# The opening of a long-convolution kernel: k's first chunk and its taps placed ahead of the filter, and kv transposed in 16-bit instead of 32-bit words

## The chip, the cores and the metric

One core of a Trainium2 chip runs the whole program. The metric is the device time of one execution in microseconds (us), median of several runs. The engines are named as in the profile: PE (TensorE matmul, with PEld for its weight loads), DVE (VectorE), ACT (ScalarE), POOL (GpSimd) and SP (SyncE, which only issues DMAs here). ACTq, DVEq and SPq are the instruction queues of those engines.

## The reference

Inputs are q, k, v (1 x 2048 x 512, bf16), a tap filter shift_k (512 x 4), a long filter ssm_k (512 x 2048), a vector ssm_D (512), and the weights w1 (512 x 1376), w2 (1376 x 512).

```python
k_shift = sum over t of k_pad[:, t:t+S, :] * shift_k[:, ks-1-t]   # 4 causal taps per channel
kv = k_shift * v
y  = irfft(rfft(kv, 2S) * rfft(ssm_k, 2S))[:S] + kv * ssm_D       # long causal convolution
h  = x + layernorm(x) * y                                          # x = q
h2 = h + relu(layernorm(h) @ w1) @ w2
```

The result is h2, in bf16.

## The kernel before, in words

The convolution is a transform of length 4096 in two stages of matmuls, 64 x 64, for the filter and for kv alike, with channels spread over the 128 partitions in four groups of 128 (`DC` = 4). The order of the instructions on each engine is written out by hand (`manual_schedule`); a framework adds the semaphores. PE works through these steps, in this order:

1. Transposes of ssm_k (`to_rows`, L246, on `sk`): eight groups of eight 128x128 transposes of 16-bit data. Each group fills one buffer of PSUM (`pst`) and is copied to `kfl` by DVE or ACT in turn (the letters "DADADADA", L291).
2. Eight rounds (L315 to L319). Round `gb` first computes one tap group (`taps`, L303): for a chunk of 512 tokens `c = gb // 2` and half of the channels, 8 matmuls of `kT` with diagonal matrices `wdiag` into `pkv`, and DVE multiplies the result by `vT` in two instructions (L310). The products kv go into `sk`, whose old content is used up by then, in pairs of neighbouring tokens. Then stage 1 of the filter for group `gb` (`stage1`, L252): 64 small matmuls into two buffers, copied to `a1k` by ACT, or by ACT and DVE in odd groups. After groups 0, 2 and 4, ACT also computes a piece of the cosine table `c2c` (`cc_part`, L210); the first of its four pieces comes ahead of step 1.
3. Transposes of kv (L337 to L349): each pair of 16-bit tokens is taken as one 32-bit word, so 32 transposes do; DVE copies a buffer as int32 words, ACT as 16-bit values in two instructions. The result is `xfl`.
4. Stage 2 of the filter (L281, L283, buffers `ps2k`, result `kf`), stage 1 of kv (`a1x`), the products of the spectra (L398), the inverse transform (L528 and L592), and the two layers of the network (`ps1m`, L604; `ps2m`, L621).

Four PSUM buffers of two banks each (`psF`, tag "ps") go round among all tiles of steps 1 to 4. A tile takes the buffer that was used four tiles earlier and waits until that one has been copied out.

SP issues, one after the other: ssm_k into `sk` (L95), then for each chunk `c` a transposing DMA of k (`kT`, L111 and L113) and one of v (`vT`, L114). ACT's queue issues shift_k (`wsh`, L97) and ssm_D (`draw`, L102) first. POOL builds `wdiag` from an identity and `wsh` (L222), then the small tables `f1hi` and `f1lo` that stage 1 multiplies by, and the negated sine table `c2n` (L229). DVE computes the turns (integers, `tsn` and `tcs`) from which ACT makes the tables by its sine function; `tcs`, the cosine's, is computed ahead of all copies (L206). `dm_f` (L205), a small table for the inverse, is the last that ACT makes before the cosine's first piece. `a1k` and later large tiles share one slot of SBUF, `slotA`: what is written into it waits for the readers of what was there before.

## Time and profile before

| | |
|---|---|
| median of 3 runs | 218.69 us (217.52 to 219.26) |
| profiled execution, its own time | 217.52 us |
| its span, first to last instruction | 215.7 us |
| granted TensorE clock | 1.000 |
| PE busy | 194.0 us (90%) |
| DVE, ACT, POOL busy | 143.3, 115.8, 79.4 us |
| ssm_k, issue to landing | 8.2 us |
| k chunks, v chunks, median issue to landing | 6.6, 5.7 us |

The profile shows one execution. Busy time of an engine counts only where that engine is what others wait for; the chain that ended last follows the work back from the last instruction and says at each step what released it. Times of instructions are counted from the start of the span. The time of an execution is somewhat longer than its span, since it includes what lies before the first and behind the last instruction that the profile records.

### The profile page before, as it was taken

The page shows a single profiled execution, that of the slowest core. Times are in us where ns is not written, and L with a number is a line of the kernel's source. Part 1 is how long each engine was busy: PE and PEld are TensorE (multiplying, and loading weights), DVE is VectorE, ACT ScalarE, POOL GpSimd, SP SyncE. Part 2 cuts the span into 40 slices and gives each one's busy share as a digit, 9 for nine tenths or more (in the row PEclk, how much of TensorE's full clock was granted, in tenths as well). Part 3 has the DMA queues.
Part 4 walks back from the last instruction along what each step waited for, and adds up shares of the span by engine and source line. Part 5 has one row for each costly group of instructions (what it writes and reads, how often), then busy time and mean ns, then how long its engine had stood idle before and what let it go on. Part 6 is the DMA issues. An engine that isn't in the chain of part 4 may idle for free.

```text
span 215.7 us, 5459 instructions
## 1 busy us (share of the span) xinstructions
PE 194.0 (90%) x2251; PEld 137.2 (64%) x2267; DVE 143.3 (66%) x236; ACT 115.8 (54%) x177; POOL 79.4 (37%) x120
## 2 busy tenths in 40 slices
PE   0399879899997999998998999999999999999992
PEld 0385434799986899996998944654646644444451
DVE  7965756976697999998495991988395470243031
ACT  2976848745697788883997048202450047016400
POOL 3299992000002999995747702110201010002000
PEclk9999999999999999999999999999999999999999
DMA  6999950000000006809950799494462430010012
GB/s 194 317 208 197 154 127 3 5 5 0 0 5 3 0 3 173 269 14 214 178 100 0 266 148 148 79 185 95 85 114 52 100 79 3 24 49 24 0 47 55
DMA packets 49513, 20.08 MB, mean 93 GB/s; under 512 B 44400, under 2 KB 47952, under 8 KB 49488
## 3 DMA queue, kind: packets, MB, share of 16 engines
q1 hardware_dynamic: 46816, 18.18, 41.4%
q10 hardware_dynamic: 2672, 1.54, 2.5%
q8 instruction: 18, 0.29, 0.6%
q14 instruction: 7, 0.06, 0.1%
HBM read 7.08 MB, written 2.10 MB: 43 GB/s over the span
## 4 chain that ended last, share of the span: by engine, by line
PE 83%; DVE 9%; DMA 4%; issue 2%; ACT 1%; DVEq 0%; ACTq 0%
PE ps1m L604 18%; PE ps2m L621 18%; PE psi L528 7%; PE psy L408 7%; PE pkv L307 7%; PE pz L592 5%; DVE a1x L241 4%; DMA sk<-in_A_ssm_k_dram 4%; PE ps2k L281 3%; PE ps2k L283 3%; PE u L281 3%; PE u L283 3%; PE pst L249 3%; PE ps L265 3%; PE pst L340 2%
## 5 line engine op out<-in xcount | busy, mean ns | idle before, releaser
L606 ACT ACTIVATE h1T<-ps1m 128x512 bf16<-128x512 f32 (+1 forms) x44 | 26.0, 596 | 55.4 <-PE ps1m L604 55.4
L621 PE MATMUL ps2m<-w,h1T 128*128 128x512 bf16 (+2 forms) x179 | 38.6, 366 | 0.6 <-issue 0.3
L604 PE MATMUL ps1m<-xT,w 128*128 128x512 bf16 (+1 forms) x176 | 38.8, 379 | 0.3 <-DVE xT L577 0.3
L624 DVE SCALAR_TENSOR_TENSOR o<-ps2m,rstd,xh 128x512 bf16<-128x512 f32 (+1 forms) x17 | 12.1, 719 | 31.2 <-PE ps2m L621 29.0
L604 PEld LDWEIGHTS <-w 128*128 128x128 bf16 (+1 forms) x176 | 17.4, 100 | 20.6 <-DVE xT L577 0.5
L621 PEld LDWEIGHTS <-h1T 128*128 128x128 bf16 (+1 forms) x187 | 17.9, 98 | 19.2
L398 POOL TENSOR_TENSOR t<-usb,kf 128x320 fp32r<-128x320 f32 x32 | 28.3, 953 | 2.0 <-ACT usb L394 1.7
L398 DVE TENSOR_TENSOR t<-u,kf 128x704 fp32r<-128x704 f32 x32 | 26.7, 886 | 3.1 <-ACT usb L394 3.0
L478 POOL TENSOR_SCALAR rstd<-mv 128x4 f32<-128x4 f32 x8 | 2.3, 283 | 67.4 <-DVE mv L476 67.4
L474 DVE BATCH_NORM_STATS2 st<-xh 128x6 f32<-128x512 bf16 x32 | 19.7, 678 | 0.0
L239 ACT CAST kf<-psy 128x512 fp32r<-128x512 f32 x30 | 17.6, 647 | 1.9 <-PE psy L408 0.3
L592 PEld LDWEIGHTS pz<-ecore,ax 32*128 32x128 f32 x512 | 15.0, 186 | 3.4 <-ACT ax L239 1.3
L574 DVE TENSOR_TENSOR qT<-pz,qT 128x1024 bf16<-128x1024 f32 x8 | 9.8, 1222 | 10.9 <-PE pz L592 6.5
L592 PE MATMUL pz<-ecore,ax 32*128 32x128 f32 (+7 forms) x512 | 15.7, 273 | 1.1 <-ACT ax L239 1.1
L239 ACT CAST a1k<-ps 128x1024 fp32r<-128x1024 f32 x12 | 12.4, 1079 | 6.7 <-PE ps L265 6.7
L408 PE MATMUL psy<-t,ipos 128*128 128x512 f32 x48 | 16.0, 393 | 0.0
L528 PE MATMUL psi<-dre,kf 128*128 128x256 f32 x64 | 15.8, 287 | 0.0
L249 PE MATMUL pst<-ident,sk 128*128 128x128 bf16 x64 | 6.9, 297 | 9.5 <-DMA sk<-in_A_ssm_k_dram 9.0
L528 PE MATMUL psi<-dim,kf 128*128 128x256 f32 x64 | 15.4, 282 | 0.0
L307 PE MATMUL pkv<-kT,wdiag 128*128 128x512 bf16 x56 | 14.8, 381 | 0.4
L239 ACT CAST ax<-psi 128x1024 fp32r<-128x1024 f32 x13 | 12.5, 1016 | 4.6 <-DVE st L474 3.0
L310 DVE TENSOR_TENSOR sk<-pkv,vT 128x512 bf16<-128x512 f32 x16 | 10.3, 687 | 6.9 <-PE pkv L307 6.8
(116 smaller groups left out, 389.4 us busy)
## 6 DMA issues: line engine op xcount, KB each, us to landing
sk<-in_A_ssm_k_dram SPq DMA_DIRECT2D x1, 2048.0 KB, 8.2
xh<-in_A_q_dram SPq DMA_DIRECT2D x16, 128.0 KB, 3.1
out_dram<-o SPq DMA_DIRECT2D x60, 32.0 KB, 1.6
w<-in_B_w_dram SPq DMA_DIRECT2D x1, 1376.0 KB, 6.0
w<-in_B_w_dram ACTq DMA_DIRECT2D x1, 1280.0 KB, 6.2
xh<-xT SPq DMA_TRANSPOSE x8, 3.3
w<-in_B_w_dram ACTq DMA_DIRECT2D x1, 96.0 KB, 6.2
draw<-in_A_ssm_D_dram ACTq DMA_DIRECT2D x2, 32.0 KB, 8.2
```

The costliest lines, as they stand in the source:

```text
L239: nc.scalar.copy(out=o, in_=i)
L249: nc.tensor.transpose(out=pst[:, 0, i, :], in_=src[:, :, :, 8 * q + i], identity=ident[:])
L281: nc.tensor.matmul(out=ps[:, kk, :], lhsT=at_k1(w_re, k1), rhs=a_in[:, k1, :], start=True, stop=False, skip_group_check=True)
L307: nc.tensor.matmul(out=ps[:, i, :], lhsT=wdiag[:, 2 * h + i, j, :], rhs=kT[c][:, 2 * h + i, 16 - j:CH + 16 - j], start=(j == 0), stop=(j = ...
L398: eng.tensor_tensor(out=t[:, :, j, :], in0=in0.unsqueeze(1).to_broadcast([P, 2, n, 2]), in1=kfr[:, :, j, ks], op=ALU.mult)
L408: nc.tensor.matmul(out=psy[:], lhsT=m_[:], rhs=t_.rearrange("p j k -> p (j k)"), start=first, stop=not first)
L474: nc.vector.bn_stats(out=st[:, i, :], in_=src[:, i, :])
L528: nc.tensor.matmul(out=ps[:, i // 2, i % 2, :], lhsT=kf[:, c, 4 * m:4 * m + 4, :].rearrange("p r k -> p (r k)"), rhs=d[:].rearrange("p d a ...
L592: nc.tensor.matmul(out=pz[:, rg, 32 * jl:32 * (jl + w)], lhsT=ax[rows, 64 * rho + n2, :, :].rearrange("p d g -> p (d g)"), rhs=ecore[q][ro ...
L604: nc.tensor.matmul(out=ps1[:fsz, :].rearrange("p (i t) -> p i t", i=4), lhsT=w1[:, c, fc * P:fc * P + fsz], rhs=hT[sc][:, :, c, :], start= ...
L606: nc.scalar.activation(out=h1T[:fsz, fc, :], in_=ps1[:fsz, :], func=ACT.Relu)
L621: nc.tensor.matmul(out=ps2[:, 0:w], lhsT=h1T[:ksz, fc, i * P:(i + 1) * P], rhs=w2[:ksz, fc, ds], start=(fc == 0), stop=(fc == NFC - 1))
```

## The change

- `wsh` is issued by SP, ahead of all else; then k's first chunk, then ssm_k, then the rest as before.
- POOL builds `wdiag` before it clears `f2hi` and `f2lo`.
- The two tap groups of chunk 0 run ahead of the transposes of ssm_k. ACT copies their results to a new tile, `ahead`, which lies in `slotA`. DVE multiplies them by v among its copies of `kfl`, behind groups 4 and 6.
- The turns of the cosine table come behind the transposes' copies on DVE, and its four pieces behind stage 1's groups 1, 2, 4 and 6 on ACT.
- Rounds 0 and 1 hold stage 1 alone. In rounds 2 to 7 one DVE instruction multiplies a whole tap group, and the products are written over v, in `vT`, which is one tile now.
- kv is transposed from there by `to_rows`, as ssm_k is: 64 transposes of 16-bit data, and eight copies.
- Small matters: the turns of `dm_f` are made from a range of their own (`r3`), and `f1d` is a tile of its own.

```diff
-    nc.sync.dma_start(out=sk[:], in_=A_ssm_k.rearrange("(c p) t -> p c t", p=P))
-    nc.scalar.dma_start(out=wsh[:], in_=A_shift_k.rearrange("(r p) j -> p r j", p=P))
+    nc.sync.dma_start(out=wsh[:], in_=A_shift_k.rearrange("(r p) j -> p r j", p=P))
...
-    vT = [vp.tile([P, DC, 512], BF16, name=f"vT{c}") for c in range(4)]
+    vT = vp.tile([P, DC, S], BF16, name="vT")
...
             nc.sync.dma_start_transpose(out=kT[c][:, :, 16:CH + 16], in_=k_d[0:CH, :])
+            nc.sync.dma_start(out=sk[:], in_=A_ssm_k.rearrange("(c p) t -> p c t", p=P))
...
-    nc.vector.tensor_single_scalar(out=tcs[:], in_=tsn[:], scalar=2048.0, op=ALU.add)
-    wrap(tcs[:], 8192)
...
+    def taps_mm(c, h):
+        ps = bank2("pkv")
+        for i in range(2):
+            for j in range(KS):
+                nc.tensor.matmul(out=ps[:, i, :], lhsT=wdiag[:, 2 * h + i, j, :],
+                                 rhs=kT[c][:, 2 * h + i, 16 - j:CH + 16 - j], start=(j == 0), stop=(j == KS - 1))
+        return ps[:]
+
+    def taps_mul(src, c, h):
+        vv = vT[:, 2 * h:2 * h + 2, CH * c:CH * c + CH]
+        nc.vector.tensor_tensor(out=vv, in0=src, in1=vv, op=ALU.mult)
+
+    ahead = slotA.tile([P, DC, CH], F32, tag="A", name="ahead")
+    for h in range(2):
+        nc.scalar.copy(out=ahead[:, 2 * h:2 * h + 2, :], in_=taps_mm(0, h))
...
-    cc_part()
     for q in range(8):
         to_rows(skv, q, kfl, "DADADADA"[q])
+        if q in (4, 6):
+            taps_mul(ahead[:, q - 4:q - 2, :], 0, q // 2 - 2)
+    nc.vector.tensor_single_scalar(out=tcs[:], in_=tsn[:], scalar=2048.0, op=ALU.add)
+    wrap(tcs[:], 8192)
...
     for gb in range(8):
-        taps(gb // 2, gb % 2)
+        if gb >= 2:
+            taps_mul(taps_mm(gb // 2, gb % 2), gb // 2, gb % 2)
         stage1(kfl, a1k, gb, ("AA", "AD")[gb % 2])
-        if gb in (0, 2, 4):
+        if gb in (1, 2, 4, 6):
             cc_part()
...
-    kv32 = sk[:].rearrange("p c t -> p (c t)").bitcast(F32).rearrange("p (m x) -> p m x", m=32)
-    xfl32 = xfl[:].rearrange("p g d n -> p (g d n)").bitcast(I32).rearrange("p (g d m) -> p g d m", g=64, d=2)
+    kvv = vT[:].rearrange("p r (a b) -> p r a b", b=64)
     for q in range(8):
-        pst = psum.tile([P, 4, P], F32, tag="ps", name="pst2")
-        for i in range(4):
-            nc.tensor.transpose(out=pst[:, i, :], in_=kv32[:, 4 * q + i, :], identity=ident32[:])
...
+        to_rows(kvv, q, xfl, "ADADADAD"[q])
```

## The prediction, made before the result was known

> **What bounds the kernel now.** I read the page's busy shares first, then the chain that ended last (whole run, then its first 60 us in order of time), then the queues of SP, DVE and ACT over the same stretch, and the DMA view microsecond by microsecond. Busy shares and chain:

> ```profile
> PE 194.0 (90%) x2251; PEld 137.2 (64%) x2267; DVE 143.3 (66%) x236; ACT 115.8 (54%) x177; POOL 79.4 (37%) x120
> PE 83%; DVE 9%; DMA 4%; issue 2%; ACT 1%; DVEq 0%; ACTq 0%
> ```

> TensorE (PE) holds 83% of the chain, so what lengthens its work lengthens the kernel unless PE stood idle there. It stands idle in the opening, which is the only part that the change touches (columns: start, length, what):

> ```profile
> 0.72 8.24 DMA sk<-in_A_ssm_k_dram
> 9.01 4.52 PE pst L249 x40
> 13.56 1.24 DVE kfl L241
> 14.84 1.60 PE pst L249 x16
> 16.44 0.22 PE pkv L307
> ...
> 25.81 0.60 PE ps L265 x62
> 26.41 2.04 issue
> 28.45 0.20 PE ps L265 x2
> ...
> 36.38 1.48 PE pkv L307 x6
> 37.87 1.30 DVE sk L310 x2
> 39.18 0.14 issue
> 39.31 3.81 PE pst L340 x32
> ```

> Read it as a relay: ssm_k lands at 9.0; PE transposes it (to 16.4); eight rounds of taps (`pkv`) and stage 1 (`ps`) follow, with one stop of 2.04 us in which PE waits for nothing that the profile shows; the last tap product on DVE ends at 39.17; then 32 transposes of 32-bit words, and stage 2 of the kernel spectrum starts at 42.87. From there on nothing is edited, so the question is only by how much 42.87 moves. SP's queue, which decides when data arrive:

> ```profile
> 0.72 0.47 SPq L95 DMA_DIRECT2D sk<-in_A_ssm_k_dram  x1
> 1.25 7.57 SPq L111 DMA_TRANSPOSE kT<-in_A_k_dram  x1
> 8.88 2.13 SPq L114 DMA_TRANSPOSE vT<-in_A_v_dram  x1
> 11.05 3.08 SPq L113 DMA_TRANSPOSE kT<-in_A_k_dram  x1
> ```

> k's first issue takes 7.57 us where later ones take 1.4 to 3.4. It ends as ssm_k's transfer does, so I read it as waiting for room behind ssm_k.

> **Part 1: ssm_k behind k's first chunk.** SP now issues the 4 KB of taps weights (0.50 us, its price on ACT's queue), then k's chunk at 1.25, then ssm_k. The chunk's issue I take at 2.0 (the v issue at 14.17 took 2.00). A chunk landed 5.2 us at the soonest after its issue began, so this one lands at 6.4, its last packets some 1.0 earlier, at 5.4. Behind it ssm_k needs 2.10 MB at the 0.40 MB per us that the DMA view gives for 4 to 8 us: 5.2 less what its start overlaps, 4.9, and 0.9 from the last packets to the landing (8.0 to 8.96 now): 11.2. So ssm_k is 2.2 late. From below, a chunk of 0.52 MB at 0.40 MB per us costs 1.3; from above, an issue of 3.4 and then the full 8.2 of now makes it land at 12.8, 3.8 late. The value is nearer the first end since ssm_k's slow start (0.49 MB up to 4.0 us) falls under the chunk.
> For chunks themselves the trace has 0.26 to 0.27 MB per us between 9 and 11 us. [...]

> **Part 2: two of eight tap groups before ssm_k.** Each holds PE 1.84 us (taps at 16.27, stage 1 at 18.10), so 3.7 leaves the relay: **-3.7**. They need `wdiag`. Its weights landed at 9.3 now, in small packets sharing the engines with ssm_k (some 100 per us, 490 per us once ssm_k had gone). Ahead of ssm_k, 512 packets are 1.0 us after a first one at about 3.0: 4.0. POOL then builds four blocks in 4.96 us, to 9.0; the last four matmuls end at 9.9, 1.3 before ssm_k. Were the weights as late as now, taps would end at about 14.6 and cost 3.4. The two copies of the results (1.05 each on ACT, as `a1k` copies) start when `dm_f` ends at 10.7, in the place of the cosine piece that moved away, and end at 12.8; ACT's first copy of `kfl` is due at 13.1. Hidden, by 0.3.
> The seven other chunks flow from when ssm_k is through, at about 10.3; now the second chunk starts there too, so their landings stay. The first v chunk, 2.3 to 5.2 after ssm_k, is there for its product at 5.8 after.

> **Part 3: products among the copies.** DVE and ACT now copy the transposes:

> ```profile
> 13.56 1.22 DVE L241 COPY kfl<-pst 128x1024 bf16<-128x1024 bf16 x1 [0.48 <-PE pst L249]
> 15.72 1.23 DVE L241 COPY kfl<-pst 128x1024 bf16<-128x1024 bf16 x1 [0.93 <-PE pst L249]
> 16.48 1.01 ACT L239 COPY kfl<-pst 128x1024 bf16<-128x1024 bf16 x1 [1.08 <-PE pst L249]
> 18.84 2.05 ACT L239 CAST a1k<-ps 128x1024 fp32r<-128x1024 f32 x2 [1.36 <-PE ps L265]
> ```

> The last copy ends 8.5 after ssm_k's landing, while transposes end at 7.3. Today a tap group fills that gap; now stage 1 must stand: **+1.2**. The first product (1.2 us, as the 128x1024 `kf` add of 1.23) takes up the 0.93 idle ahead of DVE's last copy, the second ends at 9.4 after landing. `ahead` lies in the slot of `a1k`, so ACT's first `a1k` copy waits for that second product (9.45 in place of 9.25), and all of ACT's copies are queued behind it. It ends at 10.5. PE has done groups 0 and 1 at 9.7 and holds all four PSUM buffers, so it stands 0.8 until the first copy ends, and some 0.2 twice later (groups 2 and 6) where a buffer waits for ACT: **+1.2** with the 0.2 above.
> The cosine turns (two of 1.23) hold DVE from 9.4 to 11.9 after landing; behind them is group 1's second copy, done at 13.1, which is when group 3's taps want its buffer: nothing. The same bound for ACT: 12 copies of 1.05 and four pieces of 1.27 are 17.7 us, against 17.9 for PE (8 x 0.61, 6 x 1.84, 2.04), so ACT has hardly any cover left. POOL's moved work is off the relay: its negated table ends sooner than 26.5, and its reader starts at 42.87.

> **Part 4: the stop.** In both kernels PE has 704 instructions up to the end of group 3, where the stop is, so I keep it. Gone, it would give 1.5, ACT then setting the pace.

> **Part 5: the product itself** is one instruction of 1.2 for two that took 1.29: **-0.1**.

> **Part 6: transposes of kv as 16-bit.** 64 replace 32. `vT` is read in the steps in which `sk` is, and the last 16 of those took 1.60, 0.100 each; the first 48 took 5.33, 0.111. 64 cost 6.4 plus a start of 0.1, against 3.56 now (39.31 to 42.87): **+2.9**. From above 7.1, +3.5. From below the copies, which alternate on DVE at 1.22 and ACT at 1.01, 0.61 per eight transposes: 4.9, +1.3. I take the row of the same instruction. The copies stay hidden, and DVE's last ends as its first stage 2 result is due.
> [...]

> **Sum:** 2.2 - 3.7 + 1.2 + 1.2 - 0.1 + 2.9 = **+3.7 us**. The profiled execution took 217.52 (span 215.66 and 1.86 around it), which makes 221.2. But it is the lowest of three runs, 1.2 under their median of 218.69; from there 222.4. I forecast the middle, **221.8**.

> **Rivals.**
> *No change beyond 1%.* The stop goes (-1.5), or ssm_k is only 1.3 late (-0.9) with transposes nearer the copies' pace (-0.7): +2 or less, about 220.2. For it: a stop tied to the moment of a fetch need not return. Against: the equal instruction count.
> *Not slower.* PE runs stage 1 without standing: neither the stop (2.04) nor the two waits on copies (2.4). That is -4.4 and ends at -0.7, 217.8; from 3.8 gained on it is no longer slower. For: ACT idles 6.7 us ahead of `a1k` copies now. Against: the shared slot, and ACT's 17.7.
> *Much slower.* The 7.57 of the first k issue is its own price, not room behind ssm_k. Then ssm_k is issued at 8.9 and lands at 16 or so, 7 late in place of 2.2: +8.5, about 226.5. It decides from an issue longer than 4. Against: all other issues.

> **How the numbers follow.** Forecast 0.64, no change 0.22, not slower 0.06, much slower 0.08. The range, 219.2 to 224.6, takes in part 1's ends (-0.9, +1.6), part 6's (-1.6, +0.6) and most of the stop's; the not slower case and the longest late one lie outside. One per cent, 2.2 us, is about what three runs that spread over 1.7 tell apart: above 220.9 lie five sixths of the forecast, all of much slower and some of no change, 0.68; faster by over 1%, below 216.5, asks for more than the not slower case gives at its middle, 0.04; the rest 0.28.

> **What would show it.** Right: ssm_k landing at 10.3 to 12.8 with 16 tap matmuls done before; PE idle ahead of stage 1's first group and again ahead of group 2; the kv transposes in 6.4 to 7.1; stage 2 starting at 45.5 to 47.5; the rest of equal length. Wrong: taps ending after ssm_k lands, no stop, transposes in 5 us, or a stage after stage 2's start that changes.

## The result, and the profile after

The changed kernel takes 224.68 us (median of four runs, 223.94 to 225.31), the kernel before 218.33 in the runs beside it (217.52 to 219.26): a ratio of 1.029 [1.023, 1.034]. The forecast was 221.8. The direction was right, the size was not: +6.4 us came where about +3 was expected, and the time lies 0.1 above the upper end of the stated range. (Medians here are over all runs; the ratios leave disturbed runs out, so a ratio can differ somewhat from the quotient of the medians beside it.)

The granted clock in 40 slices, and the shares of the chain, from the page of the changed kernel:

```profile
PEclk9996679999999999999999999999999999999999
...
PE 73%; DVE 13%; DMA 5%; ACT 3%; issue 2%; SPq 1%; DVEq 0%; ACTq 0%
```

PE's share of the chain fell from 83% to 73% and DVE's rose from 9% to 13%: PE waits for DVE where it did not before. And three slices of the clock show 6 and 7 tenths, where before every slice showed 9. Neither can be read from PE's busy time, which rose from 194.0 to 200.5 us: from 26 to 28 us PE counts as busy for the whole 2.00 us, at a clock of 0.50.

The chain that ended last, up to stage 2 (start, length, what):

```profile
3.58 9.23 DMA sk<-in_A_ssm_k_dram
12.85 0.94 PE pst L248 x8
13.82 1.24 DVE kfl L240
15.10 0.87 PE pst L248 x8
15.99 1.24 DVE kfl L240
17.27 1.87 PE pst L248 x16
...
20.30 1.22 DVE vT L296
...
25.82 2.76 PE pkv L290 x6
...
43.25 5.99 PE pst L248 x64
49.24 0.17 PE ps2k L280
```

In the kernel before, the same step stands here in the chain:

```profile
43.12 0.12 PE ps2k L281
```

Stage 2 of the kernel spectrum (`ps2k`) starts at 49.24 in place of 43.12: +6.1, nearly the whole loss. (The 42.87 of the prediction is the same step in PE's own rows, where the first matmul overlaps the last transposes.) Behind it the stages have their old lengths, but for one further stop of 0.58 at 131.86. In the chain PE and DVE take turns from 12.85 to 22.65: the transposes, which ran almost without a break before, now wait twice for a copy. PE's own rows say for how long (last column: idle time before, and who ended it):

```profile
15.10 0.85 PE L248 MATMUL pst<-ident,sk 128*128 128x128 bf16 x8 [0.60 <-DVE kfl L240]
17.27 4.23 PE L248 MATMUL pst<-ident,sk 128*128 128x128 bf16 x40 [1.31 <-DVE kfl L240]
```

The waits of 0.60 and 1.31 stand ahead of the third and the fourth group of transposes, before four tiles have been given out to them. The framework decides when it builds the program which of the four PSUM buffers a tile gets, and the order is not a strict round: the tiles of groups 0, 2 and 3 lie in one buffer, so each waits until the one before it has been copied: group 2 starts at 15.10, as the copy of group 0 ends (13.82 and 1.24 long), and group 3 at 17.27, as that of group 2 ends (15.99 and 1.24). The list that the edit of experiment 5 writes out to keep the changed kernel's own buffers starts 0, 3, 2, 1, 2, 2: the two tap groups, then groups 0 to 3. The list in experiment 10 for the kernel before starts, behind one added tile, 0, 3, 2, 1, 0, 2, 0: there only groups 5 and 6 of the transposes take a buffer early, and group 6 is the one that waited, for 0.49. The sentence in the description of the kernel that a tile takes the buffer used four tiles earlier is wrong. Ahead of stage 1 PE stood another 1.30, for the last copies; that wait the prediction had.

The granted clock in the opening (columns: window, its length, PE busy and instructions, clock, DMA share, GB/s):

```profile
18.00:19.00 1.00, 1.00 (x12) 0.50 1.27 279
...
26.00:28.00 2.00, 2.00 (x6) 0.50 0.81 166
...
31.00:32.00 1.00, 1.00 (x5) 0.99 0.46 100
```

The clock is halved twice, from 17.4 to 20.8 and from 24.2 to 31.0, for some 3.4 us and for some 6.8. (These times are those of the clock's own changes in the trace; the windows of whole microseconds show them roughly.) In the second stretch six tap matmuls take 2.76 us (25.82) where the same six of the last round take 1.48 at full clock (40.47). The first stretch begins 0.1 behind the wait of 1.31; the second begins inside a wait of 0.96 (24.06 to 25.02), 1.4 behind that of 1.30. In the kernel before PE had a longer wait (the stop of 2.04 lies in this window) and kept 1.00, so a wait alone does not explain it:

```profile
26.00:28.00 2.00, 0.41 (x54) 1.00 1.37 75
```

SP's queue:

```profile
1.26 2.27 SPq L110 DMA_TRANSPOSE kT<-in_A_k_dram  x1
...
4.19 8.40 SPq L114 DMA_TRANSPOSE vT<-in_A_v_dram  x1
```

k's first issue takes 2.27 now and the v issue behind ssm_k 8.40, where k's, behind ssm_k, took 7.57 before: in both kernels the long issue is that of the transposing DMA right behind ssm_k.

### The profile page after: what moved, and what is told of

Its sections match the earlier page's. It is cut to its first block, busy times and chain, and to the rows that moved or that the text cites. A ratio compares the mean times of both kernels' runs of the same rounds, so it can differ in the third digit from the quotient of the medians.

```text
span 222.5 us, 5513 instructions
## 1 busy us (share of the span) xinstructions
PE 200.5 (90%) x2285; PEld 140.6 (63%) x2299; DVE 147.6 (66%) x226; ACT 118.8 (53%) x177; POOL 83.7 (38%) x120
## 4 chain that ended last, share of the span: by engine, by line
PE 73%; DVE 13%; DMA 5%; ACT 3%; issue 2%; SPq 1%; DVEq 0%; ACTq 0%
PE ps1m L594 17%; PE ps2m L611 17%; PE pkv L290 6%; PE psy L398 5%; PE pz L582 5%; PE pst L248 4%; DVE a1x L240 4%; DMA sk<-in_A_ssm_k_dram 4%; PE ps2k L280 3%; PE ps2k L282 3%; PE u L280 3%; PE u L282 3%; PE psi L518 3%; ACT ax L238 2%; PE ps L264 2%
## 5 line engine op out<-in xcount | busy, mean ns | idle before, releaser
L594 PEld LDWEIGHTS <-w 128*128 128x128 bf16 (+1 forms) x176 | 17.4, 100 | 21.3 <-issue 0.9
L611 PEld LDWEIGHTS <-h1T 128*128 128x128 bf16 (+1 forms) x187 | 17.9, 98 | 19.2
L388 DVE TENSOR_TENSOR t<-u,kf 128x704 fp32r<-128x704 f32 x32 | 26.7, 885 | 3.1 <-ACT usb L384 3.0
L290 PE MATMUL pkv<-kT,wdiag 128*128 128x512 bf16 x58 | 18.9, 465 | 7.7 <-DMA kT<-in_A_k_dram 6.1
L290 PEld LDWEIGHTS <-wdiag 128*128 128x128 bf16 x64 | 6.8, 113 | 16.3 <-issue 6.9
L564 DVE TENSOR_TENSOR qT<-pz,qT 128x1024 bf16<-128x1024 f32 x8 | 9.8, 1223 | 10.7 <-PE pz L582 6.7
L518 PE MATMUL psi<-dim,kf 128*128 128x256 f32 x64 | 15.3, 281 | 0.0
```

The costliest lines, as they stand in the source:

```text
L290: nc.tensor.matmul(out=ps[:, i, :], lhsT=wdiag[:, 2 * h + i, j, :], rhs=kT[c][:, 2 * h + i, 16 - j:CH + 16 - j], start=(j == 0), stop=(j = ...
L388: eng.tensor_tensor(out=t[:, :, j, :], in0=in0.unsqueeze(1).to_broadcast([P, 2, n, 2]), in1=kfr[:, :, j, ks], op=ALU.mult)
L518: nc.tensor.matmul(out=ps[:, i // 2, i % 2, :], lhsT=kf[:, c, 4 * m:4 * m + 4, :].rearrange("p r k -> p (r k)"), rhs=d[:].rearrange("p d a ...
L594: nc.tensor.matmul(out=ps1[:fsz, :].rearrange("p (i t) -> p i t", i=4), lhsT=w1[:, c, fc * P:fc * P + fsz], rhs=hT[sc][:, :, c, :], start= ...
L611: nc.tensor.matmul(out=ps2[:, 0:w], lhsT=h1T[:ksz, fc, i * P:(i + 1) * P], rhs=w2[:ksz, fc, ds], start=(fc == 0), stop=(fc == NFC - 1))
```

## The account

Both kernels, cut at the same events up to stage 2 (us; events from the timelines and the chains, which differ by up to 0.07):

| piece | before | after | difference | predicted |
|---|---|---|---|---|
| ssm_k: first transpose at | 9.01 | 12.85 | +3.84 | +2.2 |
| two tap groups out of the relay | 3.68 | 0 | -3.68 | -3.7 |
| from there to stage 1, group 0 | 7.25 | 9.95 | +2.70 | +1.2 |
| group 0 to the taps of round 2 | 1.23 | 2.22 | +0.99 | +0.8 |
| those taps to stage 1, group 3 | 4.58 | 7.11 | +2.53 | +0.2 |
| group 3 to the last product | 13.36 | 11.08 | -2.28 | +0.1 |
| last product to stage 2 | 3.95 | 6.03 | +2.08 | +2.9 |
| sum | | | +6.18 | +3.7 |

(The 7.25 is 9.09 less one tap group of 1.84, the 1.23 is 3.07 less the other; both tap groups stand in the second row.) The sum is within 0.1 of the shift of stage 2's start. The theory to test had four parts: ssm_k's arrival, shared buffers, the halved clock, and 16-bit transposes. The rival was that the loss is one of these alone, and that the stops, which sit at other places in each kernel, make the rest.

## The experiments

In all of them the work of the reference is done in full; where matmuls are added, nothing reads what they write. Each ratio is against runs of the kernel before on the same chip.

**1. kv16_alone: the 16-bit transposes without the move.** The kernel before, with products written over v and `to_rows` on `vT`.

```diff
-                nc.tensor.transpose(out=pst[:, i, :], in_=kv32[:, 4 * q + i, :], identity=ident32[:])
+        to_rows(kvv, q, xfl, "ADADADAD"[q])
```

> The kernel before with one part of the change alone: kv in vT, one product per tap group, 64 transposes of 16-bit data in place of 32 of 32-bit words. ssm_k still lands first. Theory (the transposes' share of the loss is their count on PE): the changed kernel took 5.99 us for its 64 where the kernel before took 3.56 for its 32, so 2.2 to 2.6 slower than before, and the stop of 2.04 us in stage 1's group 3 stays as it is: ratio 1.010 to 1.012. Rival (they hide behind copies that wait anyway, or the early order makes them dear): below 1 us, ratio under 1.005, or more than 3.5 us.

Measured: 222.80 us, ratio 1.016 [1.008, 1.024]. Its chain:

```profile
23.32 0.84 issue
...
30.26 2.63 PE pkv L304 x6
...
47.47 0.17 PE ps2k L281
```

Stage 2 starts 4.35 later than before (43.12), and the transposes with their start are 1.9 of it: 7.19 from the last product's start at 40.28 to 47.47, where it took 5.25 from 37.87 to 43.12. The rest is not theirs, and the ratio lies above the 1.012 expected: a stop of 0.84 at 23.32 (0.09 before), one tap group at half clock (29.2 to 32.6 us) behind the stop of 27.22 (2.63 for six where 1.46 is normal), and transposes of ssm_k that start 0.4 later.

**2. ahead_alone: the move without 16-bit transposes.** The changed kernel with kv in pairs in `sk`, as before. `vT` stayed one tile.

> The changed kernel with the other part alone: k's chunk and its taps ahead of ssm_k, but kv in pairs in sk and 32 transposes of words. Since sk is read until the last transpose, the two products of the early taps come behind all copies of kfl on DVE, in four instructions of 0.69. Theory (late ssm_k 3.8, standing and clock, less two tap groups): 3.5 to 5 us slower than before, the products' place costing about 1 of it. Rival (the two parts hurt each other and each alone is small): within 2 us of before.

Measured: 230.18 us, ratio 1.053 [1.045, 1.061]: a miss, which says nothing on the move. DVE's row shows why (idle before in brackets):

```profile
30.14 1.90 DVE L301 TENSOR_TENSOR sk<-ahead,vT 128x512 bf16<-128x512 f32 x3 [7.86 <-issue]
```

The first of the four instructions for the early products ran at 21.39; the next stood 7.86 us. The trace names no releaser; it started 4.58 us after v's last chunk was issued (25.56), near the 4.8 that a chunk took at the least in the changed kernel, so I read it as a wait for that chunk. With v in four tiles this wait is gone (next).

**3. ahead_pairs: the same with v in four tiles.**

```diff
-    vT = vp.tile([P, DC, S], BF16, name="vT")
+    vT = [vp.tile([P, DC, 512], BF16, name=f"vT{c}") for c in range(4)]
```

> ahead_alone again, with v in four tiles as in the kernel before: there the second product of the early taps waited until v's last chunk had landed at 30 us, which is no part of the question. k's chunk and its taps ahead of ssm_k, kv in pairs and 32 transposes of words, the products of the early taps behind all copies of kfl. Theory: the changed kernel less 2.2 for the transposes, and 1 to 1.7 more for the products' place: 4.5 to 6 us slower than before. Rival (without the 16-bit part the early taps pay): within 2 us of before.

Measured: 221.65 us, ratio 1.010 [1.003, 1.017].

```profile
21.57 2.51 DVE sk L297 x4
...
46.49 0.22 PE ps2k L279
```

By the ratio that is some 2.2 us, less than the 4.5 to 6 expected and just above the rival's 2. The move alone is no gain, and rather a loss: the two tap groups saved are given back in the opening, where stage 2 starts 3.4 later than before. Two more things are in it: the products stand behind all copies (2.51 us), and the granted clock was halved from 18.8 to 29.0 us. Of the stops of the kernel before, none stands in its chain up to stage 2. With experiment 1 the two halves come to 1.0 + 1.6% against 2.9% for both.

**4. after_turns: the changed kernel with its buffers strictly in turn.**

```diff
-    psum = pl.push("psF", bufs=4, space=PSUM)
+    psum = pl.push("psF", bufs=1, space=PSUM)   # and tag=f"ps{n % 4}" for tile n, where it was tag="ps"
```

> The changed kernel with the four PSUM buffers taken strictly in turn. In the changed kernel the transposes' groups 0, 2 and 3 were given one and the same buffer, so that PE stood for two DVE copies (0.60 and 1.31 us). Theory A (PE's standing there also let the granted clock fall to 0.5): the standing goes, 1.5 to 2 us, the clock stays at 1.0 in 17 to 31 us and the tap matmuls of groups 2 and 3 take 0.24 in place of 0.43 each, another 2 to 2.5; if the stop of 2 us in group 3 comes back, the sum is 2 less: 1.5 to 4.5 us faster than the changed kernel. Theory B (the clock falls with the transposes themselves): only the standing goes, 1.5 to 2 us faster, taps still at 0.43.

Measured: 223.15 us, ratio 1.018 [1.010, 1.025]. PE's rows and the end of its opening:

```profile
13.20 5.95 PE L255 MATMUL pst<-ident,sk 128*128 128x128 bf16 x64 [1.34 <-DMA sk<-in_A_ssm_k_dram]
```

```profile
24.94 2.69 PE pkv L297 x6
...
47.16 0.17 PE ps2k L287
```

The 64 transposes of ssm_k run through in 5.95 us without a wait, and stage 2 starts at 47.16, 2.1 sooner than in the changed kernel, though ssm_k landed 0.35 later. So the waits were the buffers' doing. The clock fell all the same (halved from 20.6 to 27.4 us, 2.69 for six taps), as theory B had it: waits among the transposes are not needed for that. Some of the gain went again: the two early products, for which ACT's first `a1k` copy waits, took 1.61 and 2.06 us on DVE in place of 1.22 each; what slowed them was not traced.

**5. after_busy: the changed kernel with its own buffers, and 13 matmuls of 512 columns added behind groups 1, 2 and 7 of the transposes.**

```diff
+            nc.tensor.matmul(out=pst[:, 1, :, :].rearrange("p i x -> p (i x)").bitcast(F32), lhsT=wdiag[:, 0, 0, :],
+                             rhs=kT[0][:, 0, 16:CH + 16], start=True, stop=True)
```

> The changed kernel with its own buffers, and 13 matmuls of 512 columns added where PE stands: 3 behind transposes' group 1, 5 behind group 2, 5 behind group 7. Their results go into an unused bank and are read by nobody. Theory A (standing lowers the clock): granted clock 1.0 through 17 to 31 us, taps of groups 2 and 3 at 0.24 each, 2 to 2.5 us faster than the changed kernel, or no faster if the stop of 2 us comes back. Theory B (the clock does not depend on it): no gain, taps at 0.43, and 0 to 1 us slower by the added matmuls.

Measured: 226.60 us, ratio 1.038 [1.031, 1.046]. In the profiled execution the granted clock was 1.00 through the whole stretch (in the other runs 0.98 to 1.00 on average), and the tap groups from 31.1 us on took their 1.84 us, so with this work added the clock held:

```profile
26.00:28.00 2.00, 0.38 (x1) 1.00 1.48 119
```

The time did not fall. The added matmuls put stage 1 off (24.2 in place of 22.8 us), and a stop came:

```profile
26.82 2.20 issue
```

**6. base_smooth: the kernel before, buffers in turn, and 32 matmuls of 256 columns while PE waits for ssm_k.** A base without shared buffers on which single parts can be priced.

```diff
+    wps = bank2("warm")
+    for _ in range(32):
+        nc.tensor.matmul(out=wps[:, 0, 0:256].rearrange("p (b x) -> p b x", x=P), lhsT=ident[:],
+                         rhs=ident[:].unsqueeze(1).to_broadcast([P, 2, P]), start=True, stop=True)
```

> The kernel before with its four PSUM buffers taken strictly in turn and 32 matmuls of 256 columns (identity by identity, result read by nobody) on PE before ssm_k lands. They add 64 instructions ahead of PE's others, so that the place of the 2.04 us stop (instruction 704) is reached 64 instructions earlier in the work, inside stage 1's group 3 rather than at its end. [...] Rival (the stop is not tied to the count of instructions): 0.5 to 1 us faster, and a stop of 2 us stays somewhere in stage 1.

Measured: 215.99 us, ratio 0.986 [0.978, 0.993]. The transposes run through (9.32 to 15.27), and two stops of 0.41 and 0.72 stand where one of 2.04 was.

**7. smooth_kv16: base_smooth with the 16-bit transposes.**

> base_smooth with kv transposed as 16-bit data and one product per tap group, nothing else: the price of that part without stops and without a lower clock. Theory: 64 transposes in 5.9 us for 32 in 3.8, product 0.07 shorter: 2.0 to 2.2 us slower than base_smooth. Rival (the copies of xfl, longer on DVE and ACT, come on top): 3 us or more.

Measured: 220.30 us (ten runs, 218.0 to 222.2), ratio 1.006 [1.002, 1.011]. Chains of base_smooth and of this kernel:

```profile
37.23 3.80 PE pst L351 x32
41.03 0.12 PE ps2k L288
```

```profile
35.77 5.91 PE pst L256 x64
41.69 0.17 PE ps2k L288
```

From the last product, which starts at 35.80 and at 34.49, to stage 2: 5.23 and 7.20, so the part costs +2.0 by itself, as expected. Its median lies 4.3 above that of base_smooth, which is the rival's figure; but the rival's cause is not in the chain, where the 64 transposes run through without a wait for a copy. The profiled execution has a stop of 2.05 at 122.63 that base_smooth does not have at that length (0.65 at 123.94), and the runs scatter by 4 us. It is one of the fastest, at a mean clock of 0.998; five others show 0.990 to 0.992 and take 219.6 to 220.8. One stretch of 3.4 us at half clock in 218 would lower the mean by 0.008.

**8. smooth_late: base_smooth with ssm_k behind k's first chunk.** `wsh` on SP, k, then ssm_k; taps where they were.

```diff
-    nc.sync.dma_start(out=sk[:], in_=A_ssm_k.rearrange("(c p) t -> p c t", p=P))
...
             nc.sync.dma_start_transpose(out=kT[c][:, :, 16:CH + 16], in_=k_d[0:CH, :])
+            nc.sync.dma_start(out=sk[:], in_=A_ssm_k.rearrange("(c p) t -> p c t", p=P))
```

> base_smooth with only the order of the loads changed: weights of the taps, k's first chunk, then ssm_k on SP; the tap groups stay behind the transposes. The price of the late ssm_k by itself. Theory: ssm_k lands at 12.6 to 12.9 in place of 9.0 to 9.4, everything behind it moves by as much, 3.5 to 3.9 us slower than base_smooth, up to 0.7 more if PE's idle 4 us let its clock fall. Rival (other work, the table's turns on DVE above all, fills the wait): under 3 us.

Measured: 220.01 us, ratio 1.007 [1.002, 1.011]; 4.0 above base_smooth.

```profile
3.48 8.93 DMA sk<-in_A_ssm_k_dram
12.46 6.39 PE pst L256 x64
```

The first transpose moves from 9.32 to 12.46, +3.1. ssm_k needs 8.93 us from its issue, and 8.55 when nothing went ahead of it: the chunk does not absorb its start. The transposes take 6.39 in place of 5.95, since the clock was halved from 11.9 to 15.3 us behind PE's idle time; shorter stops give 0.7 back, and stage 2 starts 2.7 later (41.03 to 43.74). What makes up the rest of the 4.0 in the median was not traced; the two profiled executions differ by 2.4.

**9. smooth_after: the changed kernel, buffers in turn, and five matmuls behind the last transposes.** All but the change itself taken away.

> The changed kernel with its PSUM buffers strictly in turn and 5 matmuls of 512 columns behind the transposes' group 7 (read by nobody), so that neither a shared buffer nor, as far as these keep PE busy, a lower clock weighs on it. To be read against base_smooth (215.99), which is the kernel before with the same two helps. Theory (late ssm_k and PE standing for copies cost more than two tap groups taken out, and 16-bit transposes cost 2): 3 to 5 us slower than base_smooth, 219 to 221, clock 1.0 from 17 to 31 us or one window of 0.5 at most. Rival (the change as meant is no loss and only buffers and clock spoilt it): within 1.5 us of base_smooth.

Measured: 223.98 us, ratio 1.023 [1.017, 1.029], a miss. Clock 1.00 from 18 to 32 us, ssm_k's transposes in 5.94 without a wait, and yet:

```profile
28.24 2.31 issue
...
47.18 0.17 PE ps2k L293
```

Less its stops (2.31 here, 0.48 at 24.70) stage 2 would start at 44.4. In experiment 6, where the buffers go in turn as well, the clock is 1.00 and the change is left out, it starts at 41.03 with stops of 0.41 and 0.72, so at 39.9; in experiment 11 at 40.62 with a stop of 0.61, so at 40.0. That is 4.4 to 4.5 for the change without shared buffers, without a halved clock and without stops. Up to 0.5 of it are the added matmuls, which hold the last copy back: `a1k`'s first copy starts at 21.52 where the second product, done at 21.03, would have let it go. So 3.9 to 4.5, near the 3.7 of the prediction's sum, which held clock, stops and buffers equal; but partly by chance, since arrival is 3.2 to 3.4 here (9.32 and 9.15 to 12.54) where 2.2 was taken, and the transposes are 2.0 where 2.9 was.

**10. before_count: the kernel before with eight small matmuls, 16 instructions, at 3 us.** They end long before ssm_k lands; what they change is the count of PE's instructions.

> The kernel before with its own buffers and 8 small matmuls (identity by identity, 128 columns, 16 instructions, read by nobody) on PE at 3 us, where it is idle. They shift the count of PE's instructions by 16 and do nothing else. [...] Rival (the stop belongs to the time or to the state of the DMA queues): a stop of 2 us stays at about 26 us, and no gain.

Measured: 216.79 us (seven runs, 216.4 to 217.1), ratio 0.989 [0.986, 0.993].

```profile
26.15 0.53 PE ps L272 x54
26.68 0.43 issue
```

In the kernel before, the stop stands behind 62 matmuls of that group and lasts 2.04 us; here it stands behind 54 and lasts 0.43. The eight matmuls and their eight weight loads moved it by eight matmuls and theirs: the place went by the count. A smaller stop, of 0.09 behind six matmuls of stage 1's group 2 in the kernel before, moved by eight as well and grew to 0.31. Stage 2 starts 1.25 sooner (41.87), which is half of the gain in the median. Part of the rest may be the clock: four of the runs that the ratio counts for the kernel before show a mean clock of 0.990 or 0.991 and take 219.5 to 220.6, and none of the seven here is under 0.995.

**11. base_smooth2: base_smooth with 24 added matmuls in place of 32.**

> base_smooth with 24 added matmuls in place of 32, so 48 instructions in place of 64. [...] Rival: as base_smooth or worse, with stops of 0.4 to 0.7 as there.

Measured: 215.84 us (215.2 to 216.1), ratio 0.985 [0.981, 0.990]. It beats both kernels, and is not told apart from experiment 6. Its chain runs from ssm_k to stage 2 with one stop, of 0.61 at 20.33, though its transposes took 6.47, and its mean clock was 0.988:

```profile
40.62 0.12 PE ps2k L288
```

## Why the prediction was right or wrong

**Right.** The two tap groups gave their 3.7. Their cover held, in part by luck: PE did the 16 matmuls at 6.11 to 11.90, 0.95 before ssm_k, where 9.9 was reckoned; had ssm_k come at the 11.2 of the prediction, they would have ended behind it. `wdiag` was done at 9.86 for 9.0, and ACT's copies of the results ended before its first `kfl` copy. The wait for the second product through the slot of `a1k` cost 0.96 where 0.8 was worked out. The long first issue (7.57) went with standing behind ssm_k, as read, and the rival "much slower" fell by its own sign (2.27, under its limit of 4). The kv transposes came by the row of the same instruction, though shorter: 64 in 5.99, 0.094 each, where 0.100 was taken; with the start and the shorter gap ahead of them +2.1, not +2.9. Experiments 1 and 7 give +1.9 and +2.0 for it.

**Part 1 was mis-sized: 2.2 taken, 3.84 measured.** The step that failed is "The value is nearer the first end since ssm_k's slow start (0.49 MB up to 4.0 us) falls under the chunk". The transfer took 9.23 us from its issue, against 8.24 with nothing ahead of it. By the DMA view the chunk's small packets fill the time up to about 5.5 us, as the prediction had it (0.22, 0.21 and 0.20 MB in the microseconds from 3, 4 and 5, nearly all packets under 512 bytes); ssm_k's large ones follow with 0.26 MB in the microsecond from 6 and 0.38 in the next. So the slow start did not fall under the chunk: it was paid behind it. The landing at 12.81 is the upper bound given (12.8, 3.8 late), but that it fits so well is luck, since the bound was made of an issue of 3.4 and a transfer of 8.2, and these were 2.27 and 9.23. In smooth_late the same order alone cost 3.1 in the trace.

**Part 3 rested on a false reading of the buffers: 1.2 taken, 2.70 measured.** "The last copy ends 8.5 after ssm_k's landing, while transposes end at 7.3" assumes transposes as dense as before. Three of the first four groups shared one buffer, and the waits of 0.60 and 1.31 for their copies put the last transposes and copies that much later. The order of the buffers is fixed when the program is built and can be listed before any run; the prediction took the trace of before, where it showed in one wait of 0.49 alone, for a rule. after_turns shows it: with the buffers in turn stage 2 starts 2.1 sooner.

**The clock had no term: 0.2 taken, 2.53 measured** for the stretch from round 2's taps to group 3. No row of before showed less than 1.00 in this stretch, and I gave no price to PE standing more. after_busy shows that it is the clock: at 1.00 a tap group is back at 1.84. That the standing around groups 0 to 2 drives it is likely but not shown: in after_turns, with less standing, it fell as well. (Of the 2.53, two times 0.22 is the gap behind the first tap matmul of a group, 0.05 at full clock.)

**Part 4: the stop was kept, and it went.** "In both kernels PE has 704 instructions up to the end of group 3, where the stop is, so I keep it." The place was right as a place, its length was not. In the changed kernel PE came to that count out of the stretch at half clock and stood nowhere; the stretch behind group 3 shows -2.28. "No change" named this, but priced it at -1.5, alone, as if it came without the cause that took it away. In after_busy and smooth_after, at full clock, stops of 2.20 and 2.31 are back, the latter at that count, the former 256 instructions sooner. So the lost clock and the missing stop are likely one thing in part: 2.53 lost and 2.28 gained.

**The sum.** Arrival (+1.6) and shared buffers (+1.5) were missed by 3.1 together; clock (+2.3) and stop (-2.4) nearly cancel; the wait for the slot was 0.2 longer, and the transposes were 0.8 too dear. That is +2.4 net, and 3.7 becomes 6.1. The range failed since it took in part 1's upper end, but no cost for the order of the buffers. The rival, one part alone, falls: with the buffers in turn 1.8% are left, without the move 1.6, without the 16-bit transposes 1.0.

**Open.** What makes a stop long is not settled, nor what sets the clock. Transposes alone were on PE when it came back in smooth_late: it went from 0.50 to 1.00 at 15.3 us, while PE did nothing but ssm_k's transposes from 12.46 to 18.85, after 3.2 us of idle time.

```profile
12.00:14.00 2.00, 1.54 (x15) 0.50 1.03 232
14.00:16.00 2.00, 2.00 (x23) 0.67 1.15 190
16.00:18.00 2.00, 2.00 (x25) 1.00 1.05 231
```

Whether transposes count for less than other matmuls is not shown. The clock's four changes in the opening of the changed kernel lie 3.42, 3.41 and 6.83 us apart, one or two times 3.41. That stretches of this length decide is only my reading. In such stretches of the traces, 1.97 us of transposes came before a halving in after_turns (17.2 to 20.6), while the clock stayed at 1.00 behind 1.58 us of taps and stage 1 in smooth_after (26.7 to 30.1) and behind 1.98 in the kernel before (24.4 to 27.8). These are few, and 1.43 us of taps and stage 1 came before a halving in kv16_alone (25.8 to 29.2). The median of smooth_kv16 is 4.3 above base_smooth where its own part accounts for 2.0; a stop, as its profile shows one, and a stretch at half clock, as the mean clocks of five of its runs suggest, are the likely rest.

## What to carry to other kernels

Work brought ahead of a large load did not run for free in its shadow: the load's full time, slow start and all (9.23 us from its issue, 8.24 before), began again behind what was put ahead of it. The gain is what the load covers less what it loses, and here 3.7 saved met 3.8 lost. Before costing waits on a pool of buffers, list which buffer each tile really gets; here a pool of four held three of the first four groups in one. When a few microseconds in a dense stream of small matmuls are at stake, look for stops that the chain calls "issue" and shift the count of instructions before believing that an edit made them: here 16 more instructions left 0.43 of a stop of 2.04.

## What the runs showed of the hardware

**DVE and POOL took longer side by side.** With POOL's `wdiag` moved to the start, DVE's integer steps beside it took 1.61 and 1.66 us, where the same steps took 0.89 and 0.82 before, and `wdiag` itself took 6.76 in place of 4.96:

```profile
4.52 1.61 DVE L183 TENSOR_SCALAR w_ts<-w_ts 128x1408 int32<-128x1408 int32 x1
```

```profile
3.10 6.76 POOL L155 TENSOR_TENSOR wdiag<-ident,wsh 128x512 bf16<-128x512 bf16 x4
```

The two integer steps behind these took 1.21 and 1.01 us, 0.49 and 0.23 before; in ahead_alone, after_turns and after_busy, which also build `wdiag` early, they took 1.21 and 1.01 again. That these two engines slow each other is argued from the overlap alone. It cost nothing here, since all of it ended before ssm_k landed; had DVE been on the chain there, the 0.72 and 0.84 that the first two steps took longer would have counted.
